# A fourth chunk's transposition leaves TensorE, a weight factor moves to ScalarE, and the written-out order is searched again

## The chip, the cores and the metric

The kernel runs on one core of a Trainium2 chip. The core has five engines with a queue of instructions each: TensorE (PE: matrix products; PEld in the profile is its loading of the stationary operand), VectorE (DVE), ScalarE (ACT), GpSimd (POOL) and SyncE (SP), which here issues all DMA transfers. Each works off its own queue in order, and waits where its data or its buffer come from another engine. The metric is the device time of one execution in microseconds. Most executions of a kernel agree within 0.3%.

## What is computed

The reference chains a gated linear attention and a two-layer block, all in 32 bits, with batch 4, 8 heads, 768 tokens, 48 values per head (384 in all) and 1536 hidden values:

```python
for t in range(S):                                   # 768 tokens, per batch and head
    state = alpha[:, :, t, :, None] * state + k[:, :, t] (outer) v[:, :, t]
    y[:, :, t] = q[:, :, t] @ state
x = y.transpose(0, 2, 1, 3).reshape(B, S, H * D)     # (4, 768, 384)
mu, var = mean and variance of x over its 384 values
xn = (x - mu) / np.sqrt(var + 1e-06) * g_ln
out = x + np.maximum(xn @ w_ch1, 0.0) @ w_ch2        # w_ch1 384x1536, w_ch2 1536x384
```

`w_ch1` and `w_ch2` arrive as 64-bit floats, all else as 32-bit floats.

## The kernel before, in words

**Chunks.** The 768 tokens are cut into six chunks of 128 (`c` = 0 to 5); with four batches (`b`) there are 24 blocks. `attention(c, b)` does one: logarithm of alpha, running sums as a product with a triangle (`lps`), exponentials, scaling of k and q on VectorE (`qk`), their transposition to `kT` and `qT`, scores (`aps`), masking into `at`, update of the state (`sums`, `mid`, `st`), and the output `yps`, which ScalarE copies to `x`. Then `x` is normalized to `xn` on ScalarE (on VectorE in chunk 0) without the factor g, and `xn` is transposed into `xT_of[c]`, the operand of the first layer.

**Two ways to transpose.** With `c < BY_DMA` (2) for q and k, and `c < X_BY_DMA` (4) for x, TensorE transposes: for x three 128x128 products with the unit matrix into a PSUM tile `xps` (line 530), which VectorE (chunk 0) or ScalarE (others) copies to `xT` (line 532). In later chunks VectorE transposes blocks of 32x32 in place (`xr`, line 536), four DMAs write the blocks to a DRAM tile `xd` in transposed places (line 540), and one DMA reads it back into `xT` (line 543).

**Weights.** Each weight matrix comes in six pieces of 768 values per partition (`pieces`: six of w1, then six of w2; turns `A` to `L`). `take_weights(i)` loads a piece as 64-bit words into one of three staging buffers `ws`, and `round_weights(i)` makes 32-bit floats of it. VectorE takes the fraction out (lines 219 and 221) and the exponent bits (line 223), ScalarE shifts and clamps the exponent (line 227), VectorE joins sign and exponent to a power of two (line 229), and then multiplies fraction and power. For w1 that last step also multiplies g, one value per row of w1; a row block has its own column of `g_part`, so there are three instructions of 256 columns (line 233). For w2 it is one instruction of 768 columns (line 236).

**The layers.** Chunk 0 is done plainly (`hidden`, line 567, and `project`, line 579). Chunks 1 to 5 use schemes of sums and fewer products. First layer: sums of blocks of w1 (`combine_first`) and of xT (`combine_x`, line 834), 15 products instead of 18 (`hidden_product`, line 857), then additions of the products into `hT` on VectorE and GpSimd, and the maximum with zero on ScalarE (line 907). Second layer: sums of blocks of w2 (`combine_weights`) and hT (`combine_hidden`, line 670), 20 products instead of 24 (`product`, line 683), additions into `ob` on VectorE (lines 693 and 696) and GpSimd (line 699), and the output DMA (`send`, line 558).

**The order.** Nothing is scheduled by a compiler. Every part is a Python generator, called a turn; each `yield` ends a step. `ORDER` is a string, and each of its letters runs the next step of one turn: `a` to `x` are the 24 attention blocks, `A` to `L` the weight pieces, `Y` `Z` `P` `Q` chunk 0's layers, `S` and `W` the sums of weights, `X` and `N` those of x and hidden values, `1` and `2` the two halves of the first layer's products, `R` and `U` the maxima, `M` the second layer, `O` the reloading of x. So the string fixes the order of the instructions on each engine, and of the DMAs in SyncE's queue; the waits between engines follow from the data.

```python
    with tc.manual_schedule():
        for turn in ORDER:
            next(turns[turn], None)
```

Of the kernel before, what the change touches and what calls it, by code (L numbers as in the profile page):

```python
# [11 lines left out]
FP32 = mybir.dt.float32  # L12
# [4 lines left out]
AOP = mybir.AluOpType  # L17
# [1 line left out]
EPS = 1e-6  # L19
STAGED = 3  # L20
BY_DMA = 2
X_BY_DMA = 4
SPLIT = 4
AHEAD = 2
G = 32
# [5 lines left out]


ORDER = (
    "bacabcadaacbcaadbcadabcababbebaccbadbaaBbccaedcbceAeeaaacbfecfBcdafddeaedbdeafae"
    "bcdccbfgadhAdcgCcdbebeebfhggdfgbfffbCdcgfgecdfchgdfhgabcddchdhAiiegjhacehedhhjfg"
    "biAdfidAeBhBijffYYiCjZZYYifZYlZCgjYDlYYjjZZYBZYgDieEgDgDjZZekEhZYGZgZigZGeeYgYgg"
    "fZYEhfGfkChihiYFYijfgEhgkhFZYhgYfghijgkFeZZlGZShfZYHlhHfYFYZeZHelYiZgllPmZkJIgJk"
    "PeiYjJIflHeSZIQgkIlYSjiPkffennSQlOKjLSnSjmSQhKnSjLnKPkiljnhSQnLkkjkWknkShOmPhkhl"
    "kOOhWlmmphmQmkmXjWQnXjlSQjPmkilXSXkP2OXWjXQjkjW2iXoSWX2oWX22Pi2mnol1j1mom2omSpoo"
    "l1XSpk2oW2m112p1m2pm11m1W211pp12O122r22jnn21lpnmnjSml1riOn2l12Rl111kqS1m21W1Rkp2"  # L40
    "o21mUXpq1mU2rUrnmj1rl2Rno2oomqonrormpokO1rNM2Mipin1op1ionoqUM2qp2W12RkMmNqiMoRtk"
    "UrpkqNM1NoMliMlNUMMNMNMKNqMlNorMWrnmtltNRMsqppMWNMriMMMpNlsqqqnoqttNttMtMsXMMssM"
    "sMNMNMX1oXXppMvstM2MXMMNMsppXoMXoqMsMMXM1nqqv11Xq1trMq2tqX21rn12v1r2ur2r222rvsqs"
    "svsu1rs1nuvvt2s11ss11p22rtsvosn2uropuXru222221uts212stnU1211u1121222Op1Rp2tRU21R"
    "Us1pXqU11x2tO2MM1vwMUM12xuRvu1vurNNNNwtOuuMwRxvNtxRNutwwMM2MOwNXwMNuXMMtNM1rMMMw"
    "qtXMMMxNUNxtMMsNMMMxXxMtXtrMMqMNrMXNvutMMwNuMMMNMMMxMLMOM11vvuq2X2O2wMus1wX11222"
    "2r2Xt1222w22utsqxvw2x2ww1vx21sX12121xwvq2O2x2w111u1uvU121w12s1wuRvx12U11J1q21R1U"
    "OvRxU121wMMu2xxsRNMw2NNMRM1MUNN2MMuUMqXN1MrNNRMNvMXNXMMMM2MMMxNM1uNXMMNMNMOXMXMv"
    "MMXOMMMXxNxwxMMvNMMMMMXMx21w1x222212v12w222x122w2212X11UX2212121121121wx111MU11X"
    "2RR2v1211212211R1URU211XOUM2XNRX1MX1RM2MXN2MXNXNMXXMXMMMN111U1MN1M1122MNM1MM2MM1"  # L50
    "11NNN121O11NM1MM21N1112N1122M1MMM12MM12N222M22M2RM1M2N22MM2MU1ON2M22M2UURR22RNNM"
    "MNM1MMOMRMNMUUM2ONMNNNMO2MMMUMNMMMMMRMMNNMMMNMNMMNMMMMMMMMNMNMMMMMMM"
)


# [1 line left out]
def kernel(  # L57
# [36 lines left out]
    nc = tc.nc  # L94
# [9 lines left out]
    NJ = DF // P  # L104
# [81 lines left out]
    g_part, zero_col = small[:, NF + 2:2 * NF + 2], small[:, 2 * NF + 2:]  # L186
# [22 lines left out]
    def round_weights(i):  # L209

        dst, _ = pieces[i]
        ws = staged.pop(i)
        words = ws.bitcast(INT32).rearrange("p a (c t) -> p a c t", t=2)
        lo, hi = words[:, :, :, 0], words[:, :, :, 1]
        ts, stt = nc.vector.tensor_scalar, nc.vector.scalar_tensor_tensor
        ts(out=dst.bitcast(INT32), in0=hi, scalar1=0x000FFFFF, scalar2=0x00100000,
           op0=AOP.bitwise_and, op1=AOP.bitwise_or)  # L220
        stt(out=dst, in0=lo.bitcast(UINT32), scalar=2.0 ** -32, in1=dst.bitcast(INT32),  # L221
            op0=AOP.mult, op1=AOP.add)
        ts(out=lo, in0=hi, scalar1=0x7FF00000, scalar2=None, op0=AOP.bitwise_and)
        yield
        if i == 0:
            nc.scalar.mul(g_part, g_col, 2.0 ** -20)
        nc.scalar.activation(out=lo, in_=lo, func=AFT.Relu, scale=8.0, bias=least)
        yield
        stt(out=hi, in0=hi, scalar=-(1 << 31), in1=lo, op0=AOP.bitwise_and,
            op1=AOP.bitwise_or)  # L230
        if i < NJ // 2:
            for f in range(NF):
                stt(out=dst[:, f], in0=dst[:, f], scalar=g_part[:, f:f + 1],
                    in1=hi[:, f].bitcast(FP32), op0=AOP.mult, op1=AOP.mult)
        else:
            stt(out=dst, in0=dst, scalar=2.0 ** -20, in1=hi.bitcast(FP32),  # L236
                op0=AOP.mult, op1=AOP.mult)

    def take_weights(i):
        if i < STAGED:  # L240
            load_weights(i)
            yield
        if pieces[i][1].dtype != FP32:
            yield from round_weights(i)
        yield
        load_weights(i + STAGED)
        yield
# [50 lines left out]
    def attention(c, b):  # L298
# [226 lines left out]
        if c not in xT_of:  # L525
            xT_of[c] = work.tile([P, NF, B, P], FP32, name="xT", tag="xT")
        if c < X_BY_DMA:
            xps = ps.tile([P, NF, P], FP32, name="xps", tag="bank", bufs=6)
# [440 lines left out]
```

## Time and profile before

| | |
|---|---|
| median of 3 runs | 420.69 us (420.14 to 421.5) |
| the profiled execution | 420.64 us |
| its span, first to last instruction | 418.9 us |
| busy TensorE / VectorE / ScalarE / GpSimd | 409.0 / 351.4 / 178.0 / 153.2 us |
| granted TensorE clock | 1.00 |
| moved by DMA | 59.52 MB, 133741 packets |

Busy times are unions of the instructions' intervals. Matrix products are pipelined: the duration of one (381 ns for 128x256) is longer than the distance to the next in a stream, so a busy TensorE need not be one at its peak. A 32-bit product appears as two records in the profile, a transposition as one. An engine that is idle away from the path that ends last costs nothing.

### The profile page before, as it was taken

How to read it: one execution, taken by the hardware profiler on the slowest of the kernel's cores; microseconds unless marked ns; L12 is line 12 of the kernel's file. 1: busy time of each engine (PE TensorE's matmuls, PEld its weight loads, DVE VectorE, ACT ScalarE, POOL GpSimd, SP SyncE). 2: the span in 40 equal slices, each digit the busy share in tenths (PEclk: the TensorE clock that was granted, in tenths of full speed). 3: DMA queues.
4: the chain of work that ended last, by engine and by line, in shares of the span. 5: the costliest groups of instructions: out<-in, count | busy, mean ns of one | idle time of the engine just before them, and what ended most of it. 6: DMA issues, size and time to landing. Idle time of an engine off the chain costs nothing.

```text
span 418.9 us, 11553 instructions
## 1 busy us (share of the span) xinstructions
PE 409.0 (98%) x4608; PEld 360.9 (86%) x4608; DVE 351.4 (84%) x713; ACT 178.0 (42%) x440; POOL 153.2 (37%) x169
## 2 busy tenths in 40 slices
PE   6998999999999999999999999999999999999996
PEld 4787888766678889998889999889998899999996
DVE  3999999999999989996888996688876767977873
ACT  5498456724243496414546612364313242014110
POOL 3011000003203990043395033493152940499123
PEclk9999999999999999999999999999999999999999
DMA  7998889987778778587784546433035200001201
GB/s 247 325 297 246 206 201 293 287 194 181 145 221 176 200 167 185 128 195 178 146 215 70 130 105 166 88 95 77 0 114 104 67 1 2 0 20 38 94 20 56
DMA packets 133741, 59.52 MB, mean 142 GB/s; under 512 B 90764, under 2 KB 129804, under 8 KB 133688
## 3 DMA queue, kind: packets, MB, share of 16 engines
q1 hardware_dynamic: 133688, 58.79, 55.1%
q8 instruction: 36, 0.59, 0.6%
q14 instruction: 17, 0.14, 0.1%
HBM read 42.17 MB, written 16.61 MB: 140 GB/s over the span
## 4 chain that ended last, share of the span: by engine, by line
PE 89%; DVE 4%; ACT 2%; DMA 2%; issue 1%; SPq 1%; POOL 0%; POOLq 0%; DVEq 0%
PE hps L857 31%; PE ops L683 30%; PE ops L579 8%; PE hps L567 8%; PE aps L405 3%; PE yps L463 3%; PE yps L467 2%; PE sums L432 2%; DMA rq<-in_q_dram 2%; PE xps L530 1%; PE tps L355 1%; PE aps L397 1%; PE lps L407 1%; SPq L132 1%; DVE w L221 0%
## 5 line engine op out<-in xcount | busy, mean ns | idle before, releaser
L699 POOL TENSOR_TENSOR ob<-ob,u 128x192 f32<-128x192 f32 x40 | 26.3, 668 | 64.5 <-DVE ob L696 48.3
L857 PE MATMUL hps<-sum,w 128*128 128x256 f32 x192 | 46.3, 381 | 0.0
L907 ACT ACTIVATE hT<-hT 128x512 f32<-128x512 f32 x48 | 28.8, 624 | 34.9 <-POOL hT L879 18.5
L447 POOL TENSOR_TENSOR mid<-mid,gate 112x192 f32<-112x192 f32 x20 | 11.4, 568 | 80.0 <-DVE mid L445 33.3
L683 PE MATMUL ops<-w,hT 128*128 128x192 f32 x224 | 40.5, 327 | 0.0
L857 PEld LDWEIGHTS hps<-sum,w 128*128 128x128 f32 x192 | 36.1, 190 | 5.0
L683 PEld LDWEIGHTS ops<-w,hT 128*128 128x128 f32 x224 | 37.1, 190 | 0.7 <-issue 0.2
L857 PE MATMUL hps<-xT,w 128*128 128x256 f32 x136 | 34.0, 380 | 0.0
L579 PE MATMUL ops<-w,hT 128*128 128x384 f32 x96 | 33.0, 491 | 0.0
L567 PE MATMUL hps<-xT,w 128*128 128x256 f32 x144 | 32.5, 382 | 0.0
L567 PEld LDWEIGHTS hps<-xT,w 128*128 128x128 f32 x144 | 27.0, 190 | 4.2
L683 PE MATMUL ops<-ws,sum 128*128 128x192 f32 x160 | 28.7, 327 | 0.0
L857 PEld LDWEIGHTS hps<-xT,w 128*128 128x128 f32 x136 | 25.5, 190 | 3.1
L683 PEld LDWEIGHTS ops<-ws,sum 128*128 128x128 f32 x160 | 26.5, 190 | 0.3
L579 PEld LDWEIGHTS ops<-w,hT 128*128 128x128 f32 x96 | 17.6, 190 | 10.7 <-DVE w L236 0.3
L693 DVE TENSOR_TENSOR ob<-ops,ob 128x192 f32<-128x192 f32 x50 | 17.3, 353 | 10.6 <-PE ops L683 6.5
L447 POOL TENSOR_TENSOR st<-st,gate 112x192 f32<-112x192 f32 x16 | 11.7, 729 | 37.3 <-DVE st L445 25.9
L683 PE MATMUL ops<-ws,hT 128*128 128x192 f32 x128 | 23.6, 328 | 0.0
L463 PEld LDWEIGHTS yps<-st,qT 48*64 48x64 f32 x320 | 19.9, 134 | 4.0 <-issue 2.0
L467 PE MATMUL yps<-vx,at 64*64 64x48 f32 x320 | 22.7, 219 | 0.0
L463 PE MATMUL yps<-st,qT 48*64 48x48 f32 x320 | 22.0, 220 | 0.6 <-ACT x L493 0.6
L405 PEld LDWEIGHTS aps<-qT,kT 48*64 48x64 f32 x576 | 19.0, 134 | 4.1 <-issue 0.8
(255 smaller groups left out, 1134.2 us busy)
## 6 DMA issues: line engine op xcount, KB each, us to landing
ws<-in_moe_w_ch_dram SPq DMA_DIRECT2D x12, 768.0 KB, 5.9
td<-tr SPq DMA_DIRECT2D x64, 96.0 KB, 3.1
vn<-in_v_dram SPq DMA_DIRECT2D x12, 384.0 KB, 4.3
kept<-x SPq DMA_DIRECT2D x20, 192.0 KB, 3.0
ob<-kept SPq DMA_DIRECT2D x20, 192.0 KB, 3.1
out_dram<-ob SPq DMA_DIRECT2D x19, 192.0 KB, 1.9
ra<-in_alpha_dram SPq DMA_DIRECT2D x16, 192.0 KB, 2.6
kT<-td SPq DMA_DIRECT2D x32, 96.0 KB, 4.2
```

The costliest lines, as they stand in the source:

```text
L405: nc.tensor.matmul(to, kT[rs, p, s], qT[rs, p, s], start=True, stop=True)
L432: nc.tensor.matmul(up[h, p], qk_of(c, b)[ts, 1, p, i, :h.stop - h.start], vn[ts, i, p], start=True, stop=True)
L447: nc.gpsimd.tensor_mul(new, new, by)
L463: nc.tensor.matmul(yps[i][halves[s], i, p], qT[rs, p, s], (now, mid)[s][rs, p], start=True, stop=r != i)
L467: nc.tensor.matmul(yps[r][halves[s], i, p], at[halves[r], p, s], by, start=r != i, stop=True)
L567: nc.tensor.matmul(hps, w1[:, j // 2, f, j % 2 * P:][:, :P], xT_of[0][:, f, bs], start=(f == 0), stop=(f == NF - 1))
L579: nc.tensor.matmul(ops_of[b], hT_of[c][:, j, b], w2[:, j], start=(j == 0), stop=(j == NJ - 1))
L683: nc.tensor.matmul(acc, lhs[:, j], rhs[:, j], start=(j == 0), stop=(j == NT - 1))
L693: nc.vector.tensor_add(x, acc, x)
L699: getattr(nc.gpsimd, f"tensor_{op}")(x, x, y)
L857: nc.tensor.matmul(acc[:, i], w, b, start=True, stop=True)
L907: nc.scalar.activation(out=x, in_=x, func=AFT.Relu)
```

## The change

Three things are changed. x of chunk 3 is no longer transposed by TensorE, but in the second way, as chunks 4 and 5 were. In `round_weights` for the pieces of w1, ScalarE multiplies g into the power of two (three instructions of 256 columns), and VectorE then multiplies fraction and power in one instruction of 768 columns, as for w2; two more steps (`yield`) stand around ScalarE's part. And `ORDER` is a new string, different from its fourth letter on, one line longer, so that lines of the changed kernel below it have numbers higher by one.

```diff
-X_BY_DMA = 4
+X_BY_DMA = 3
...
 ORDER = (
-    "bacabcadaacbcaadbcadabcababbebaccbadbaaBbccaedcbceAeeaaacbfecfBcdafddeaedbdeafae"
-    "bcdccbfgadhAdcgCcdbebeebfhggdfgbfffbCdcgfgecdfchgdfhgabcddchdhAiiegjhacehedhhjfg"
...
-    "MNM1MMOMRMNMUUM2ONMNNNMO2MMMUMNMMMMMRMMNNMMMNMNMMNMMMMMMMMNMNMMMMMMM"
+    "bacOabbccbaadbbacacacbacbdaacbabdadcbadacadbfacafdbdedabcfecdafCcafcBbebdcgaddab"
+    "hcbcdeffebbcebCcfeeBdeaecadhdbffcgdefagdghibcddAefbghhedgegeggchghhadAeggjhhgdci"
...
+    "U2MM2M221M2RU2RM2RMM2NNMNUMOM2NUM1MMM1MRNMMNMNNUNOMMMNMNMMMNMMNMMMNMMMMMMMMNMNMM"
+    "MMMM"
 )
...
         if i < NJ // 2:
+            yield
             for f in range(NF):
-                stt(out=dst[:, f], in0=dst[:, f], scalar=g_part[:, f:f + 1],
-                    in1=hi[:, f].bitcast(FP32), op0=AOP.mult, op1=AOP.mult)
-        else:
-            stt(out=dst, in0=dst, scalar=2.0 ** -20, in1=hi.bitcast(FP32),
-                op0=AOP.mult, op1=AOP.mult)
+                nc.scalar.mul(hi[:, f].bitcast(FP32), hi[:, f].bitcast(FP32), g_part[:, f:f + 1])
+            yield
+        stt(out=dst, in0=dst, scalar=1.0 if i < NJ // 2 else 2.0 ** -20, in1=hi.bitcast(FP32),
+            op0=AOP.mult, op1=AOP.mult)
```

More of the change, by code (lines that the diff above doesn't have):

```diff
@@ L33 @@
 ORDER = (
-    "bacabcadaacbcaadbcadabcababbebaccbadbaaBbccaedcbceAeeaaacbfecfBcdafddeaedbdeafae"
-    "bcdccbfgadhAdcgCcdbebeebfhggdfgbfffbCdcgfgecdfchgdfhgabcddchdhAiiegjhacehedhhjfg"
[L36 to L51, printed above, removed]
@@ L52 @@
-    "MNM1MMOMRMNMUUM2ONMNNNMO2MMMUMNMMMMMRMMNNMMMNMNMMNMMMMMMMMNMNMMMMMMM"
+    "bacOabbccbaadbbacacacbacbdaacbabdadcbadacadbfacafdbdedabcfecdafCcafcBbebdcgaddab"
+    "hcbcdeffebbcebCcfeeBdeaecadhdbffcgdefagdghibcddAefbghhedgegeggchghhadAeggjhhgdci"
+    "AihAAeBcAeCejBfffeYfiOZBiYiZkBAYeCZjZfYZYBiCYDZZCEDlDZDYYYEjlfjZDghjZfiEZYZggDeY"
+    "jZefEigYChkZYjeGYgEfYZGhFeieGgEhZfFkYFiFhgZZHOYhZHZFYhfgkiYYZgjGFkYfSgHfjhigYlSf"
+    "hSJklHZhYlIlllIfkZiZIKfjmiQJIKJgniSePYgeQPPkLlggnPjSLkjlKLjnhSlhnnPkjmSjOnnWjiSk"
@@ new lines @@
+    "kSWnlkmQkPhkpkQliWmhmhimSmQSlmhnPhWQmXkoXWjoijlSk2XWQiP1XjXkkXlXjQ22nWj2XSWm1noX"
+    "pmimlSookjlmooo2lSpi112pXp2221mn2kk1m1m1Oi2i11m22kS12ppp22oSm11jj1121q12122X2mnj"
+    "21ijmW1m12iRn12Ur2rO1lnpoO1m2mokOlRUnlpLU2orpm2rrRmrrnq21oooq1UrnWpo2oM1MpoUlmq1"
+    "RnpRMpqlWq1sMoNMqNMslMNN1otRrnMqMNpMMnlqWlUpMMNoNrrptMMonnntNMNWkmMMMpNNqkNqqqtt"
+    "tMsttNsMMMNsMqsMNNotqMproXMMsMsMOMMXMMpMoXnMvXXsMMqX2XM1vt1qr2OrqMX1X21qu122rp1t"
+    "11o211rq12u22vrrv1rsvssr2s2vss22sos2t2vt2usu2p2pUXtv1p12u2q11Unu1sOtR122uX11O1p1"
@@ new lines @@
+    "22Uw1u1w11s1RRt2211x12v2qMMNMoRNUMM22uNMRUNNRMpxMMNuvMuuwsrvtNwMMMwNMMNwxpMutnMm"
+    "UNNuwwsMsutMqxxtXxNNMnxMrswMMMxMMNMrMMMMNvqMMMNtMXX1sMMXXXwvvMOxM1v2X2X1w2t22X12"
+    "1212r121qwM1222wxuuqwxrw2t2r22u1x2rOX1Uxwv12v2v1O12xqUv111x1t1swu11RX12t221R112U"
+    "1ROtR2vxu22sU12MM1xsRwU1NMNxrMNN2MMMN1MNNRMMNv2NMqNutwuMMxMuMtMMMxMUNXMMwxNXMMxw"
+    "MM1xMMN2NXMxMXMvXXvxNMwXvMMNMMXMMXMM1xw1221w2221v122121O2X21222wu111v21w2uU222M2"
+    "2U1211X1111O11122RRUX1211u222O1112RM1UMXXX2NMXMXNO2MXUMRNRMM1XNXN21M21M12MM21NXR"
@@ L53 @@
+    "112M2N1UM1NMMNM1MN211M1J11N1M2M11211MMM1N1OX2MMNRKMM111112R2NM22NMNMM22O2M2M22MU"
+    "U2MM2M221M2RU2RM2RMM2NNMNUMOM2NUM1MMM1MRNMMNMNNUNOMMMNMNMMMNMMNMMMNMMMMMMMMNMNMM"
+    "MMMM"
 )
```

## The prediction

> **What bounds the kernel now.** I read the page first: totals, then the forty slices.
>
> ```profile
> PE 409.0 (98%) x4608; PEld 360.9 (86%) x4608; DVE 351.4 (84%) x713; ACT 178.0 (42%) x440; POOL 153.2 (37%) x169
> ...
> PE   6998999999999999999999999999999999999996
> ...
> DVE  3999999999999989996888996688876767977873
> ```
>
> TensorE (PE) is busy nearly throughout. VectorE (DVE) is just as full from slice 2 to slice 14, and looser afterwards. So there are two stages: up to some 150 us both engines can set the pace, later TensorE alone. Next I read busy times per ten microseconds (columns: stretch, its length, then busy us of PE, PEld, DVE, ACT, POOL with counts).
>
> ```profile
> 20.00:30.00 10.00, 9.85 (x222) 8.66 (x222) 9.86 (x18) 8.87 (x27) 1.35 (x2) 1.00 1.06 295
> 30.00:40.00 10.00, 8.13 (x197) 6.87 (x189) 9.90 (x23) 9.12 (x25) 1.74 (x3) 1.00 0.96 275
> 50.00:60.00 10.00, 10.00 (x158) 8.43 (x158) 9.83 (x18) 5.53 (x10) 1.02 (x2) 1.00 0.85 177
> 110.00:120.00 10.00, 9.38 (x212) 6.70 (x212) 10.00 (x23) 1.79 (x5) 0.83 (x1) 1.00 0.79 195
> 310.00:320.00 10.00, 10.00 (x54) 9.22 (x53) 4.93 (x11) 3.52 (x7) 3.06 (x5) 1.00 0.53 118
> ```
>
> In 30 to 40 and again in 110 to 120 TensorE falls short while VectorE stands at 9.9 and 10.0: there TensorE waits for VectorE. The granted clock is 1.00. Last, the groups that the change touches, and four steps of the chain of work that ended last.
>
> ```profile
> L530 PE MATMUL xps<-consts,xn 128*128 128x128 f32 x48 | 7.8, 278 | 1.6 <-DVE xn L519 1.6
> ...
> L532 ACT COPY xT<-xps 128x384 f32<-128x384 f32 x12 | 5.5, 472 | 6.8 <-PE xps L530 6.8
> ...
> L536 DVE STREAM_TRANSPOSE xr<-xn 128x384 f32<-128x384 f32 x8 | 4.5, 568 | 0.0
> ...
> L233 DVE SCALAR_TENSOR_TENSOR w<-w,small,ws 128x256 f32<-128x256 f32 x18 | 7.7, 482 | 0.2
> ...
> L236 DVE SCALAR_TENSOR_TENSOR w<-w,ws 128x768 f32<-128x768 f32 x6 | 5.9, 990 | 0.2
> ...
> L570 ACT ACTIVATE hT<-hps 128x256 f32<-128x256 f32 x24 | 8.8, 380 | 11.1 <-PE hps L567 11.1
> ...
> L523 ACT ACTIVATE xn<-x,few 128x384 f32<-128x384 f32 x20 | 14.2, 709 | 0.7
> ```
>
> ```profile
> 159.79 0.33 PE xps L530 x3
> ...
> 115.08 0.50 ACT x L493
> ...
> 415.38 0.56 POOL ob L699
> 415.96 0.36 DVE ob L693
> ```
>
> Three transposes of x take TensorE 0.33 us in its stream (the 278 ns of one are mostly pipeline). At 115 us TensorE waits on an activation that itself came late. The run ends with a GpSimd addition that releases the last VectorE addition.
>
> **How I follow TensorE.** I add up the pitch of its instructions in their order: 432 ns for a product of line 857 or 567 (0.86 us for two in the chain), 325 at line 683, 645 at line 579, 109 for a transpose, small attention products by the length of their clusters. That gives 400.3 us of work; start minus work done is its lateness. It reads 4.6 us after the loads, 9.6 once the first weights are used (work 30 us), 10.05 at work 75, 12.1 at 115, 13.5 at 155, 15.5 at 265, and no more afterwards. I do the same for VectorE (lateness 8.7, 9.7, 10.8 and 14.2 at work 30, 75, 115 and 155) and call "lead" the VectorE work that must be done ahead of a TensorE instruction minus the TensorE work ahead of it. Lateness of VectorE plus lead is a floor under TensorE's. In the kernel before the highest lead is 0.6 us in the opening, 0.0 at work 50 to 80, and -1.1 to 0.0 from 100 to 150: VectorE is the floor all along.
>
> **The change, part by part.** (1) Chunk 3 loses four times three transposes: 12 x 109 ns = 1.3 us of TensorE work, on the path, so -1.3. Its four ScalarE copies go too (4 x 0.47 = 1.9 us), which is off the path.
>
> (2) Each of those four x gets one VectorE transposition (568 ns row; 2.2 us in all), four DMA writes and one read. They stand between TensorE work 143 and 234, where VectorE still shows gaps, so I cost them at nothing; uncovered they are 2.2 us. SyncE's queue gets 20 issues more. One takes 0.43 to 0.47 us in the lines 540 and 543; before, its densest stretch of 10 us of TensorE work holds 26 issues, after 23. From the end of normalization to the data in place it was 0.33 + 0.47 us; by the rows of chunks 4 and 5 it becomes 0.57 + 4 x 0.47 + 1.8 (landing of the write) + 0.43 + 2.7 (landing of the read) = 7.4 us. The new order pays for that by distance: the last read of chunk 3 is issued at work 233.8, the first product that needs VectorE's sums of it stands at 239.3. The way between is 0.43 + 2.7 + 2.8 us (VectorE's work from the first such sum to the last needed) = 5.9 against 5.5. But SyncE runs ahead: for chunk 4 before, it issued the corresponding read 2.7 us earlier than TensorE's lateness would put it. So about 2.2 us are to spare, and I cost it at nothing.
>
> [...]
>
> (3) Weights: per piece of w1, three VectorE products (7.7 / 18 = 0.43 us each) become one (5.9 / 6 = 0.98). 18 x 0.43 - 6 x 0.98 = 1.8 us less VectorE work, in its full stage. Against that ScalarE multiplies three times per piece between two VectorE steps, so VectorE hands over and waits. No row shows this form. Bounds for one product: 0.38 (line 570, the same width) and 0.71 (line 523, wider, with a scale per row); I take 0.43, nearer the equal width. A trip is then 3 x 0.43 + two handovers of some 0.06 = 1.4 us, at most 2.3. The new order puts other VectorE work into that gap: 0.74 us at the first piece, 1.19 at the second, 3.15, 0.93, 3.4 and 2.9 at the others. Uncovered: 0.7 + 0.2 + 0.5 = 1.4 us, bounds 0.8 and 4.1. Queued behind the waiting VectorE step are the next piece's rounding and the masks of the scores; TensorE's first hidden products wait for it.
>
> [...]
>
> (4) The order. In the opening the masks of line 411 take scores that stand 4.1 us deeper in TensorE's work than the masks stand in VectorE's; before it was 2.4. With TensorE 4.9 late there and some 0.2 us until a product is in, VectorE leaves the place 4.1 + 4.9 + 0.2 = 9.2 us late, against 8.6 at work 20 before: 0.6 more. With the trips VectorE is 2.0 us later after the opening. Its lead over TensorE is 0.5 at work 31, -0.2 at 75, -1.8 to -2.2 at 100 to 120, -3.6 at 130 to 160: in the second half of its full stage it is 1.5 to 2.6 us less in the way. Floor at 75: 9.7 + 2.0 - 0.2 = 11.5 (before 10.05). At 115: 10.8 + 2.0 - 1.8 = 11.0, at 155: 14.2 + 2.0 - 3.6 = 12.6, against 13.5 before. Net -0.9; bounds +1 (the relief meets another wait) and -2.5 (trips covered).
>
> (5) After 155 lateness rose 2.0 by short waits on ScalarE, DMA and GpSimd. The kind of work is the same, so zero, bounds +1 and -1. At the end the sums of the fourth last product stand 0.65 us further from the last one, which takes the GpSimd addition off the chain: -0.3, bounds -0.6 and 0.
>
> Sum: -1.3 - 0.9 - 0.3 = -2.5. The profiled execution took 420.64 us (span 418.9 and 1.7 around it), the median is 420.69, so no correction: **418.1**.
>
> **Rivals.** *Transposes alone:* VectorE's relief goes into another wait, and only (1) counts: 419.3. For it: 13.5 to 15.5 came from many small waits. Against: VectorE at 10.0 in 110 to 120.
>
> *ScalarE's trip decides:* products of 0.71 us, 4.1 us uncovered, VectorE 4.7 late; floor at 155 is 14.2 + 4.7 - 3.6 = 15.3, 1.8 above before; with -1.3 and -0.3 that is 420.8. For it: ScalarE at 9.12 in 30 to 40, where the first trips fall. Against: from 40 us on it is half idle.
>
> *x late, the slower case:* SyncE issues in order; a write of chunk 3 waits behind another engine, and chunk 3's first products stand. The queue's own waits show one such:
>
> ```profile
> SPq L540 <- DVE xr L536: 8.0, 2, 7.5
> ```
>
> A wait of 7.5 us on that path, less 2.2 to spare, costs 5.3: 420.64 - 2.5 + 5.3 = 423.4. It makes the kernel slower from a delay of 2.2 + 2.5 + 1.3 = 6.0 us. Against it: such waits before cost TensorE nothing.
>
> That the change does less than it says I exclude: in the order of its instructions it has 2348 matmuls for 2360, 677 VectorE instructions for 685, 426 on ScalarE for 412, 410 DMAs for 390, as counted above.
>
> **How the numbers follow.** A measurement of this kernel tells 0.3% (1.3 us) from no change: 419.4 to 421.9 is "the same". Forecast 0.54 (own range 415.7 to 419.9), transposes alone 0.15, ScalarE's trip 0.16, x late 0.15. Faster: 0.48 of the first, half of the second, 0.03 of the third, in all 0.59. Slower: x late and 0.02 of the trip, 0.17. Same: the rest, 0.24. The range reaches down to the sum of the good bounds (-1.3 - 2.5 - 0.6 - 1.0 = -5.4, 415.2) and up over the trip's case with 0.8 us of later waits: 415.2 to 421.6; most of x late stays outside.
>
> **What would show it.** Right: 36 transposes at the line of 530; TensorE 9.9 or more at 110 to 120; VectorE gaps of 0.5 to 1 us before the single weight product of the first two pieces, released by ScalarE; no wait of TensorE for x of chunk 3 near 245 us; lateness about 14.6 at the end. Wrong: products of 0.6 us or more on ScalarE; TensorE idle for over 2 us near 245 us; VectorE full up to 160 us and TensorE waiting with it.

## The result, and the profile after

The changed kernel takes 433.02 us (median of 5 runs, 431.84 to 433.66); the kernel before, run beside it, 420.72 (5 runs). The ratio is 1.0286, 95% interval 1.0259 to 1.0313: 12.3 us slower, where 2.5 us faster was predicted. The profiled execution took 433.02 us, span 431.3. In e6 and e12 below a single execution stood over 1.5% above the fastest of its kernel; their times and ratios leave it out, but the profile of e6 is of that execution.

The page of the changed kernel, totals and slices (the last row shown is the granted clock):

```profile
PE 413.5 (96%) x4596; PEld 363.7 (84%) x4596; DVE 356.8 (83%) x705; ACT 184.5 (43%) x454; POOL 154.4 (36%) x169
...
PE   7978899899989999999999999998999999999997
...
DVE  4777999999989899996999987696974798667983
...
PEclk9979999999999999999999999998999999999999
```

The instruction counts differ by the numbers predicted (12 fewer on TensorE, 8 fewer on VectorE, 14 more on ScalarE). What is new is in the slices: VectorE, full from the second slice on before, stands at 7 in slices 2 to 4, and the clock row has a 7 and an 8 where before the granted clock was 1.00. The busy times by stretch (stretch, length, then PE, PEld, DVE, ACT, POOL, clock, DMA share, GB/s) put numbers on it:

```profile
20.00:30.00 10.00, 7.08 (x135) 6.46 (x136) 6.00 (x11) 5.09 (x17) 0.95 (x1) 0.82 0.98 289
30.00:40.00 10.00, 8.21 (x162) 7.18 (x161) 7.59 (x16) 7.78 (x24) 1.29 (x1) 0.84 0.86 247
...
110.00:120.00 10.00, 10.00 (x125) 6.30 (x125) 8.94 (x17) 3.50 (x11) 2.32 (x3) 1.00 0.71 137
290.00:300.00 10.00, 7.99 (x57) 7.12 (x49) 6.88 (x17) 3.56 (x8) 5.82 (x5) 0.83 0.45 117
```

In 110 to 120 the relief that the prediction expected can be seen: TensorE 10.00, VectorE 8.94 (before 9.38 and 10.00), though this stretch of time now holds work that came some 9 us earlier before. But from 20 to 40 us VectorE is busy for 13.6 us instead of 19.8, and at 290 there is a second hole. Added up as in the prediction, TensorE is 17.2 us late after the opening (before 9.6), 22.8 at work 155 (13.5) and 28.9 at the end (15.3). About 7.6 us are lost in the opening (work 0 to 30), 1.7 more by work 155, 4.3 behind that; the 1.3 us of transposes come off.

What stands in the opening is in the chain of work that ended last (start, us, what):

```profile
20.04 7.25 DMA gate<-row
27.38 0.37 DVE st L442
...
28.68 2.74 PE tps L356 x12
31.42 1.90 PE yps L459 x32
```

A transfer of 2 KB is on the chain for 7.25 us. The gate of a block of chunk 0 is the last token's row of its running decay: that row of ScalarE's `eq` goes to DRAM as `row` and comes back as a column (`gate`), and VectorE's product `st` (line 442) needs it. SyncE's queue shows how it comes to that (start, us, issue; the first two lines are of the kernel before, the others of the changed kernel, where the third is from the chain).

```profile
7.53 1.43 SPq L334 DMA_DIRECT2D row<-eq  x2
12.80 0.37 SPq L423 DMA_DIRECT2D gate<-row  x1
...
9.84 0.43 DMA row<-eq
...
15.59 0.39 SPq L424 DMA_DIRECT2D gate<-row  x1
```

Before, the `row` of the first two blocks goes out at 7.53 and 8.72 us, ahead of the loads of chunk 1's first half (9.00 to 10.70 us, 1.2 MB), and the gates follow at 12.8, 14.7, 17.7 and 22.5 us; VectorE waits for none. In the new sequence these loads go out at 7.05 to 8.60 us, and the second `row` behind them at 9.84. The first gate waits for that row (the wait that ended last by the profile, 2.7 us) and issues only at 15.59, and SyncE, whose last issue ended at 12.84, holds everything behind it: the data engines run dry from 15 to 18 us (GB/s in slices of 1 us from 0 to 40),

```profile
GB/s 0 25 292 254 177 210 376 378 379 395 383 375 372 375 307 54 1 12 210 396 281 197 148 335 329 378 357 320 301 246 338 310 292 108 111 303 207 225 362 214
```

and then the other gates (18.3, 20.0, 21.7 us) mix with 1.2 MB of chunk 1's second half (16.1 to 17.8) and two loads of weights of 768 KB (18.8 and 20.5 us; before 13.9 and 15.1). VectorE's queue behind the waiting product holds masks, scaling and the weights' rounding; TensorE's sums of the next block wait for it (2.9 us in two pieces, the longer 2.0), because the blocks of chunk 0 use one PSUM tile for their sums, one after the other. From 26.4 to 33.3 us the granted clock is 0.50: the 12 transposes of q and k at 28.7 take 2.74 us, where 16 took 1.99 us in the kernel before:

```profile
10.36 1.99 PE tps L355 x16
```

At 293 us the waits of the stretch 290 to 298 show the second place:

```profile
ACT hT L908 <- POOL hT L896: 3.2, 2, 1.8
PEld hps L858 <- ACT x L482: 2.3, 1, 2.3
...
PE hps L858 <- ACT x L482: 2.0, 1, 2.0
```

TensorE waits for a PSUM tile that ScalarE has not yet copied to `x`; that copy stands in ScalarE's queue behind two ReLUs (line 908) that wait for GpSimd's additions.

### The profile page after: what moved, and what is told of

Its sections match the earlier page's. It is cut to its first block, busy times and chain, and to the rows that moved or that the text cites. A ratio compares the mean times of both kernels' runs of the same rounds, so it can differ in the third digit from the quotient of the medians.

```text
span 431.3 us, 11569 instructions
## 1 busy us (share of the span) xinstructions
PE 413.5 (96%) x4596; PEld 363.7 (84%) x4596; DVE 356.8 (83%) x705; ACT 184.5 (43%) x454; POOL 154.4 (36%) x169
## 4 chain that ended last, share of the span: by engine, by line
PE 87%; DMA 4%; DVE 4%; issue 1%; ACT 1%; SPq 1%; POOL 1%; DVEq 0%; ACTq 0%
PE ops L684 30%; PE hps L858 28%; PE hps L568 7%; PE ops L580 7%; PE aps L406 3%; PE sums L433 2%; PE yps L464 2%; PE yps L468 2%; DMA gate<-row 2%; PE tps L356 1%; DMA rk<-in_k_dram 1%; PE yps L459 1%; DMA xT<-xd 1%; PE xps L531 1%; SPq L133 1%
## 5 line engine op out<-in xcount | busy, mean ns | idle before, releaser
L700 POOL TENSOR_TENSOR ob<-ob,u 128x192 f32<-128x192 f32 x40 | 27.8, 706 | 60.7 <-DVE ob L697 47.9
L448 POOL TENSOR_TENSOR mid<-mid,gate 112x192 f32<-112x192 f32 x20 | 12.6, 628 | 91.4 <-DVE mid L446 69.9
L908 ACT ACTIVATE hT<-hT 128x512 f32<-128x512 f32 x48 | 28.5, 624 | 38.1 <-POOL hT L880 13.9
L580 PE MATMUL ops<-w,hT 128*128 128x384 f32 x96 | 32.6, 489 | 0.0
L580 PEld LDWEIGHTS ops<-w,hT 128*128 128x128 f32 x96 | 17.8, 190 | 10.9
L684 PEld LDWEIGHTS ops<-ws,sum 128*128 128x128 f32 x160 | 26.4, 190 | 0.3
L684 PE MATMUL ops<-ws,hT 128*128 128x192 f32 x128 | 24.8, 339 | 0.0
L684 PEld LDWEIGHTS ops<-ws,hT 128*128 128x128 f32 x128 | 22.5, 199 | 0.5
L468 PE MATMUL yps<-vn,at 64*64 64x48 f32 x320 | 22.4, 220 | 0.5 <-issue 0.5
L448 POOL TENSOR_TENSOR st<-st,gate 112x192 f32<-112x192 f32 x16 | 10.5, 658 | 33.5 <-DVE st L446 33.5
```

What stands on the lines that cost most here:

```text
L448: nc.gpsimd.tensor_mul(new, new, by)
L468: nc.tensor.matmul(yps[r][halves[s], i, p], at[halves[r], p, s], by, start=r != i, stop=True)
L580: nc.tensor.matmul(ops_of[b], hT_of[c][:, j, b], w2[:, j], start=(j == 0), stop=(j == NJ - 1))
L684: nc.tensor.matmul(acc, lhs[:, j], rhs[:, j], start=(j == 0), stop=(j == NT - 1))
L700: getattr(nc.gpsimd, f"tensor_{op}")(x, x, y)
L908: nc.scalar.activation(out=x, in_=x, func=AFT.Relu)
```

## Experiments

Two theories at the start. A: the sequence of turns loses the time, in the opening (A1: gates behind loads) and at 293 us (A5). B: one of the two code changes loses it. `OLD` and `NEW` are the two strings of turns; ratios are to the kernel before, run in the same rounds.

**e1 and e1b: x over DRAM alone, in the old sequence.**

```diff
-X_BY_DMA = 4
+X_BY_DMA = 3
 ORDER = OLD with one turn more for each of m, n, o, p; first X of chunk 3 later
```

> The kernel before with one part of the change: x of chunk 3 goes by VectorE and over DRAM; the old sequence of turns, with one turn more for each of chunk 3's four blocks and the first combination of chunk 3's x moved some 46 turns back, behind the later arrival. Theory A (the order of turns costs the 12 us, this part gains its 12 transposes): 420.7 - 1.3 = 419.4 us, between 418.4 and 420.6. Theory B (the transfer of x is what costs): 423 us or more, with TensorE waiting for products of chunk 3 near 225 us.

431.5 us, 1.0256 [1.0203, 1.0309]: a miss for theory A. In the waits from 205 to 255 us:

```profile
DVE xr L536 <- DMA xd<-xr: 6.2, 1, 6.2
...
PE hps L857 <- DVE qk L327: 4.3, 1, 4.3
```

The second block's transposition got the buffer of the first, whose four writes stood in SyncE's queue behind `vn` and `vx`. In e1b that is mended by hand:

> Again the kernel before with x of chunk 3 over DRAM, in the old sequence of turns, but the second and third block's transposes on VectorE 18 turns apart and each block's writes issued at once behind its transpose, the first combination of x 51 turns back. In the first placement VectorE's second transpose waited 6.24 us for the buffer that the writes of the first had not yet left, and TensorE 4.41 us behind it. Theory A (that wait was the placement's, the part itself gains its transposes): 418.5 to 421.5 us, and no VectorE wait for a write of x. Theory B (a transfer of x costs wherever it stands in the old order): 425 us or more.

431.5 us again, 1.0252 [1.0202, 1.0301]. That wait is gone and others have come: the largest, 4.2 us of TensorE, is for the reads of q and k of chunk 5:

```profile
PE aps L405 <- DMA qT<-td: 4.2, 1, 4.2
```

In SyncE's queue from 216.7 to 227.7 us stand eight writes and three reads of x of chunk 3 (the writes 2.0 to 2.1 us a set of four), and the reads of q and k issue only behind them. So in the old sequence, at two hand-made placements, the way over DRAM costs 10 to 11 us. The traces show SyncE's issue time and a buffer as the waits, not the transfer (a write of x lands in 1.8 us in e1). This is the rival "x late" in another place. It is not what the changed kernel suffers: there TensorE's longest wait between 225 and 255 us is 0.2 us (a weight load), and it is for issue.

**e2: g on ScalarE alone, in the old sequence.**

```diff
         if i < NJ // 2:
+            yield
             for f in range(NF):
-                stt(out=dst[:, f], in0=dst[:, f], scalar=g_part[:, f:f + 1], ...)
+                nc.scalar.mul(hi[:, f].bitcast(FP32), hi[:, f].bitcast(FP32), g_part[:, f:f + 1])
+            yield
 ORDER = OLD with two turns more for each of A to F
```

> The kernel before with the other part alone: ScalarE multiplies g into the exponent word, in the old sequence of turns with two turns more for each of the six pieces of w1 (word and multiplication put a few turns ahead of the last product; ScalarE's exponent step of the second piece put beside that of the first). Theory A (the order costs the 12 us): between 419.5 and 422, since VectorE has 1.8 us less to do and each product waits some tenths of a microsecond for ScalarE. Theory B (ScalarE's trip is what costs): 424 us or more, the opening later by 3 us or more.

422.78 us, 1.0039 [1.0015, 1.0062]: 1.6 us slower (0.6 to 2.6), a little above A's range and far from B's 424. B falls for this part.

**e3: the new sequence alone.**

```diff
-X_BY_DMA = 3
+X_BY_DMA = 4
 round_weights as before
 ORDER = NEW without the parts' own turns
```

> The new sequence of turns with neither part: the turns that belong to the parts alone are taken out, VectorE multiplies g as before, x of chunk 3 is transposed on TensorE. Theory A (the order costs): 433.0 + 1.3 = 434.3 us, between 432.5 and 436, with VectorE waiting for the gates of chunk 0 as in the changed kernel (3 us or more in the opening) and TensorE at half clock behind it. Theory B (the parts cost): 424 us or less.

434.91 us, 1.0318 [1.0274, 1.0363]. The sequence alone has the whole loss. With both code changes in it the ratio is 1.0286, so they may gain some 1.3 us together, but the two intervals overlap. Theory A holds, with fewer gate waits than expected (1.4 us).

**e4: the old opening, the rest new.**

```diff
-ORDER = NEW
+ORDER = OLD[:162] + NEW without the turns that OLD[:162] has used
```

> The changed kernel with both parts; the first 162 turns (to about 38 us) are those of the old sequence, the rest are those of the new one in their order. Theory A1 (7.6 us are lost in the opening, by the gates of chunk 0 queued behind the bulk loads, and carried to the end): 433.0 - 7.6 = 425.4 us, between 423.5 and 427.5, with no VectorE wait for a gate and no half clock before 40 us. Rival A2 (what the opening loses is met again by later waits, the loss lies elsewhere in the order): 431 us or more.

428.55 us, 1.0171 [1.0121, 1.0221]: between the two forecasts. The gates' waits are gone, but ScalarE's product of the first piece is now bare (VectorE waits 1.4 us for line 235, TensorE 1.3 for VectorE), and a half-clock window follows at 42.9 us.

**e5, e6, e7: gates on another queue; the copy before the ReLUs; both.**

```diff
-            nc.sync.dma_start(gate[:, :ne], ...)                            # e5, e7
+            (nc.gpsimd if whole else nc.sync).dma_start(gate[:, :ne], ...)
-    "1ROtR2vxu22sU12MM1xsRw...                                              # e6, e7
+    "1ROt2vxxRu22sU12MM1sRw...
```

> The changed kernel, but the four small gate transfers of chunk 0 are issued from GpSimd's queue instead of SyncE's. Theory A1 (the opening loses its time because these 2 KB transfers stand behind 0.4 to 1.2 MB loads in one queue): VectorE waits for gates under 0.5 us (3.3 us in the changed kernel), no TensorE stall of 2.1 us near 23 us, no half clock at 26 to 33 us, and 433.0 - 5 = 428 us, between 425 and 430. Rival A3 (the data engines are full, so another queue does not help): gates land as late, 432 us or more. Rival A4 (the opening is late by its order of work on VectorE and not by the gates): gates on time, but 431.5 us or more.

> The changed kernel, but near 290 us ScalarE copies x of a block of chunk 5 out of PSUM before two ReLUs that wait for GpSimd, instead of behind them (two turns move). Theory A5 (TensorE's stall of 2.16 us at 293.3 us comes from that order, and the half clock at 296.1 to 299.5 us from the stall): both gone, 433.0 - 2.2 - 1.7 = 429.1 us, between 428 and 431. Rival: TensorE is held there by something else next (VectorE's sums, the ReLUs themselves), and less than 1.5 us is gained: 431.5 us or more.

> Both edits together: gates of chunk 0 from GpSimd's queue, and the copy of x ahead of the two ReLUs near 290 us. If the two losses are separate, the gains add: 433.0 - 5 - 3.9 = 424.1 us, between 421 and 427. If later waits take the opening's gain back, 429 us or more.

e5: 436.55 us, 1.0344 [1.0285, 1.0404], worse. GpSimd is idle, yet its first gate issues at 16.0 us, and all four are slow:

```profile
POOL gate L424 <- DMA row<-eq: 11.9, 1, 11.9
```

```profile
gate<-row POOLq DMA_DIRECT2D x4, 2.0 KB, 5.8
```

The first view is GpSimd's waits, the second the DMA issues (size, median us to landing). GpSimd waits until 16.0 us for the second `row`, the other half of the way through DRAM, issued at 10.3 us behind the same 1.2 MB of loads; and then 2 KB take 5.8 us. So rival A3 fits: from GpSimd's queue, while the data engines still moved 160 to 406 GB/s, the four gates took 5.2 to 6.8 us to land, against 4.4 by the profile of the kernel before, and VectorE waited 5.3 us for one, where it waited 3.3 us for three in the changed kernel.

e6: 430.65 us, 1.0214 [1.016, 1.0268]; the forecast was 429.1, between 428 and 431. e7: 432.38, 1.027 [1.0221, 1.0319], far from its forecast of 424.1, with the loss of e5 in it. The hole at 293 us is gone; the clean pair for its price is e8 and e9 below.

**e8, e9: loads behind the gates, without and with the copy moved.**

```diff
-            load(c + 1, b // 2, "akq")
+            load(c + 1, b // 2, "a" if (c, b) == (0, 3) else "akq")   # k, q: new turn z
-    "badacadbfacafdbdedabcfecdafCcafcBbebdcgadd abhcbc...
+    "badacadbfacafdbdedabcfecdafCcafc bebdcgaddzBabhcb...
```

> The changed kernel, but in the opening the loads of k and q of chunk 1's second half and one load of weights (1.5 MB in all) are issued behind the last gate of chunk 0 instead of ahead of three of them; all gates stay on SyncE's queue. The run with the gates on GpSimd's queue showed 5.2 to 6.8 us from issue to landing, so another queue did not help while the loads filled the data engines. Theory A1b (2 KB transfers wait behind the bytes already asked for, whatever the queue): VectorE waits for gates under 0.8 us in the opening (3.3 us in the changed kernel), no TensorE stall over 1.2 us between 20 and 35 us, and 433.0 - 5 = 428 us, between 425 and 430.5. Rival A4 (the opening is late by its order of work on VectorE): gates on time, but 431.5 us or more.

> The same, and the copy of x of a block of chunk 5 ahead of the two ReLUs near 290 us, which alone took away the stall at 293 us and the half clock behind it. If the losses are separate, 428 - 3.9 = 424 us, between 421.5 and 427; if the opening is late by its order of work, 427.5 to 430 us.

e8: 433.09 us, 1.0277 [1.0247, 1.0306], no gain. e9: 430.6, 1.023 [1.0193, 1.0268]; both missed their forecasts. Moving the copy is worth 2.5 us by the two medians, not 3.9. The intervals of the two overlap, but the ratio falls in all three pairs that differ by this copy: by 0.0047 here, by 0.0072 from the changed kernel to e6, by 0.0074 from e5 to e7. And TensorE is full there:

```profile
290.00:300.00 10.00, 10.00 (x113) 9.15 (x112) 8.23 (x18) 3.89 (x8) 7.44 (x6) 1.00 0.40 100
```

In e9 VectorE waits 0.2 us for gates instead of 3.3. Yet the first product of the hidden layer (line 568) starts at 47.6 us, after 48.3 in the changed kernel and 39.7 before. The gate's wait was removed and the time was not: VectorE now waits 4.0 us for weights (line 220), one load of which I had put behind the gates. The chain of e9:

```profile
19.69 4.42 DMA gate<-row
...
26.37 6.71 DMA rq<-in_q_dram
```

My first theory, that the gates are the cause, falls in that form: they were the wait that ended last, and others stood right behind.

**e10: everything removed that I could name.**

```diff
-ORDER = NEW
+ORDER = OLD[:162] + NEW without the turns used, copy before the ReLUs (e6); g on VectorE
```

> The first 162 turns of the old sequence, then the new one; g is multiplied by VectorE as before (the wait for ScalarE's product cost TensorE 1.42 us and a half-clock window at 41 to 46 us in the run with the old opening), x of chunk 3 goes over DRAM, and the copy near 290 us stands ahead of the two ReLUs. If the opening (7.6 us) and the place near 293 us (3.9 us) are all that the new sequence loses, 433.0 - 7.6 - 3.9 = 421.5 us, between 420 and 423.5; if the rest of the new sequence loses too, 425 us or more.

422.91 us, 1.0049 [1.0029, 1.007], inside the forecast (a second run, e10b below, came out higher). First hidden product at 40.8 us, granted clock 1.00, and no transfer among the long pieces of its chain up to 48 us.

**e11: products that fill the waits.**

```diff
+        if whole and b >= 2:
+            for _ in range(10 if b == 2 else 6):
+                nc.tensor.matmul(sums[1]...[:, :P], zero[:, :R], zero, start=True, stop=True)
...
+        if (c, r, n) == (3, 0, 12):          # ten more, the same
```

> The changed kernel with matrix multiplications that nobody reads: 10 and 6 ahead of the two products of the opening that wait for VectorE behind a gate, and 10 ahead of the product that waits at 293 us, each 128 x 112 by 128 x 128, into a bank that is free there. They fill waits and take none away. Theory C (waits of some 2 us inside one 3.41 us window halve the granted clock for the next window): no half clock at 26 to 33 us nor at 296 to 299.5 us, and 433.0 - 1.7 - 2 = 429.3 us, between 427.5 and 431. Rival (the clock is not what costs; TensorE waits as long for others): 432 us or more.

431.61 us, 1.0249 [1.0223, 1.0275]. The clock is 1.00 in both places, and one half-clock window (46.0 us) is left:

```profile
PEclk9999899999999999999999999999999999999999
```

The gain is 1.4 us where 3.7 were expected, and the interval overlaps with the changed kernel's (1.0259 to 1.0313). Over all executions, by their mean clocks, the changed kernel has 2.8 half-clock windows of 3.41 us in an execution (one lowers the mean clock by 0.004), e11 has 1.2 and the kernel before 0.3. Among executions of one kernel, each window more goes with 1.1 us more (0.8 to 1.3, from 156 executions of all kernels here). By that estimate the half clock goes with some 2.7 of the 12.3 us. It is an upper estimate, since the waits that come ahead of a half clock cost time themselves.

**e12: the bytes in another order.**

```diff
-    "badaca dbfacafdbdedabcfecdafCcafcBbebdcgadd  abhc...   (A1 some 45 turns later)
+    "badacCadbfacafdbdedabcfecdaf cafcBbebdcgaddzAabhc...   (and e6, and load as in e8)
```

> The changed kernel with the copy near 290 us ahead of the two ReLUs, and in the opening the order of the transfers changed: one load of weights goes out ahead of the first gate, into the gap of 15 to 18 us in which the data engines stood idle; k and q of chunk 1's second half and the load of the weights needed first go out right behind the last gate. VectorE's instructions keep their order. Theory B1 (the order of the bytes makes VectorE idle): waits of VectorE for gates and weights under 1 us together in the opening (3.3 us in the changed kernel, 4.0 in the run with loads behind the gates), first hidden product at 43 to 45 us instead of 48.3, and 430.6 - 4 = 426.6 us, between 424.5 and 428.5. Rival B2 (VectorE's order of work): no wait for gates or weights, but others in their place; first hidden product past 46 us and 429.5 us or more.

428.93 us, 1.02 [1.0155, 1.0244], past the upper end of B1's forecast (428.5) and under B2's 429.5; first hidden product at 45.5, between the two. No wait for weights, 1.9 us for one gate. So this run decides for neither. Its chain has again two late transfers of little data and a load:

```profile
9.93 6.11 DMA row<-eq
16.10 3.56 DMA gate<-row
...
25.89 8.81 DMA ra<-in_alpha_dram
```

**e13 and e10b: x of chunk 3 on TensorE again, beside its partner.**

```diff
-X_BY_DMA = 3
+X_BY_DMA = 4
 ORDER = e10's, m to p with two turns (transposes, copy) in place of three
```

> The variant with the old opening, g on VectorE and the copy ahead of the ReLUs, but x of chunk 3 transposed by TensorE and copied by ScalarE as before (12 transposes more). If the way over DRAM gains its transposes and costs nothing in the new sequence: 1.3 us more than the partner, so 424.2 us if that is 422.9, between 423.4 and 425. If the way over DRAM costs TensorE something there: less than 0.5 us more than the partner, or faster.

> The variant with the old opening, g on VectorE, x of chunk 3 over DRAM and the copy ahead of the ReLUs, run once more as the partner on the same chip: 422.9 us, between 422.2 and 423.7.

426.15 against 424.36 us on one chip (1.013 [1.0094, 1.0165] and 1.0085 [1.0053, 1.0117]): the way over DRAM gains 1.8 us in the new sequence behind the old opening; 1.3 were predicted. The single executions of the two spread over 2 us each, so the gain is uncertain by some 1.5 us to each side. Both times lie above their forecasts: e10b is 4.05 us over the kernel before, its twin e10 was 1.5.

**e14, e15, e16: where in the opening.**

```diff
+ORDER = OLD[:80] + ...      # e14, else as e10
+ORDER = OLD[:120] + ...     # e15
+ORDER = NEW up to the first Y + OLD's rest, neither code part   # e16
```

> The quiet variant (old opening, g on VectorE, copy ahead of the ReLUs; 422.9 and 424.4 us in two runs), but only the first 80 turns (to about 24 us) are the old ones. If the loss lies in the first 24 us (gates and order of loads): 423 to 425 us, first hidden product by 41.5 us. If it lies in VectorE's order of work behind that: 427 to 430 us, first hidden product past 44 us.

> The same with the first 120 turns (to about 31 us) of the old sequence. If the loss lies in the first 24 us, as the run with 80 turns; if it lies evenly over VectorE's order of work between 24 and 48 us, between the two, some 425 to 427 us.

> The kernel before (neither part), but up to the first hidden product its turns are those of the new sequence, the rest the old ones. If the opening's loss is the sequence's own and stays to the end: 421 + 5 to 7 = 426 to 428 us. If later work of the old sequence takes it back: 423 us or less.

e14: 426.29 us, 1.0127 [1.0099, 1.0156]; e15: 424.49, 1.0079 [1.0049, 1.011], as e10b within its interval; e16: 426.94, 1.0146 [1.0109, 1.0183], 5.3 us over the kernel before, as forecast. e14 lies between its two forecasts. With 120 turns of the old sequence the opening's loss is gone, so it is made in the first 31 us, and e16 shows that the old rest does not take it back. In e14 one load of weights came late; its issue stands at 20.45 us, as one does in the changed kernel (20.47):

```profile
20.45 9.15 DMA ws<-in_moe_w_ch_dram
```

Put together, one profiled execution each (VectorE's busy and idle time are those up to the first hidden product, from VectorE's first instruction at 0.9 us on; "on the chain" are transfers of over 3 us that land between 10 us and that product):

| kernel | first hidden product, us | VectorE busy / idle, us | transfers on the chain |
|---|---|---|---|
| before | 39.7 | 31.9 / 6.9 | none |
| e13 | 40.4 | 32.6 / 6.9 | gate 4.68 |
| e10 | 40.8 | 32.4 / 7.5 | none |
| e15 | 40.9 | 33.0 / 7.0 | none |
| e10b | 41.7 | 33.1 / 7.6 | none |
| e4 | 42.6 | 32.4 / 9.3 | v 6.64 |
| e14 | 43.4 | 32.0 / 10.5 | weights 9.15 |
| e16 | 45.4 | 33.1 / 11.5 | gate 7.21, weights 6.69 |
| e12 | 45.5 | 33.1 / 11.5 | row 6.11, gate 3.56, alpha 8.81 |
| e3 | 45.6 | 32.7 / 11.9 | v 7.49, weights 8.15 |
| e11 | 46.9 | 34.2 / 11.8 | weights 7.04, q 5.91 |
| e8 | 47.3 | 33.1 / 13.3 | v 9.09, weights 7.67 |
| e9 | 47.6 | 33.2 / 13.5 | gate 4.42, q 6.71 |
| changed | 48.3 | 33.2 / 14.1 | gate 7.25 |

Kernels with the same opening show how far one execution can be trusted: e10, e10b and e13 differ by 1.3 us, the changed kernel and e11 (the same but for the filling products) by 1.4, and not the same transfers stand on their chains. So differences of that size between rows mean nothing.

What the runs show: the opening of the new sequence makes the loss (e10 and e15 without it, e16 with it alone), and VectorE idles more there, while its work ahead of the product grows by 0.1 to 1.3 us (2.3 in e11). What is read from the traces: where the product is late, large or small transfers stand on the chain, different ones from kernel to kernel. Their lengths do not rank the kernels (e12 has the longest), and one stands on e13's chain without harm. That the transfers are the cause, and not the new order of VectorE's and ScalarE's work in the same stretch, fits the traces but was not separated: e12, the run meant for it, came out between its two theories. That the root is the second `row` at 9.84 us and the three dry microseconds behind it is read from the traces too (e12 has it: the row of 9.93 us in its chain, 16.10 its first gate); a run with that row alone moved ahead was not made.

## Why the prediction was wrong

**Step (4), the order, failed.** "0.6 more" for the opening measured 7.6. The floor under TensorE was built from VectorE's work and its lead over TensorE; no transfer was in it, and neither was a wait of VectorE. In the changed kernel VectorE idles for 7.2 us more ahead of the first hidden product, 3.3 of it directly for gates. I had compared SyncE's queue near chunk 3 and by the count of issues in its densest stretch, and not transfer by transfer in the opening, where only the string moved it. The two sequences could have been compared there without a run: in the new one the second row stands behind 1.2 MB of loads that it preceded before, and the first weights behind 1.2 MB that they preceded. Net -0.9 at work 155 was forecast with a floor of 12.6; it measured 22.8, 9.3 more than before. The half clock, which the profile of before never showed, added to it: some 2.7 us at most by the estimate at e11, and 1.4 us measured there, not clear of noise. What remains open is how much of the 7.6 is due to late transfers and how much to the new order of the engines' work around them.

**Step (5), "zero, bounds +1 and -1", failed too.** Lateness grew by 4.3 us more than before behind work 155. Moving one ScalarE copy ahead of two ReLUs gave about 2.5 us back (e8 to e9). I had called the kind of work the same; the order in ScalarE's queue was not, and I had not looked for the instruction that a late ReLU holds up. The gain of 0.3 at the end cannot be told apart here. The sum's end, 418.1, rests on these two steps; its lateness of 14.6 at the end measured 28.9.

**Steps (1) and (2) held.** 36 transposes are left; no wait for x of chunk 3; 1.8 us gained in the new sequence (e13 to e10b, uncertain by 1.5) for 1.3 predicted. "I cost it at nothing" is right only in a sequence that leaves SyncE the room: in the old one, placed by hand, it cost 10 to 11 us in e1 and e1b.

**Step (3) held in size.** The groups of the changed kernel (count, busy us, mean ns, idle before):

```profile
L237 DVE SCALAR_TENSOR_TENSOR w<-w,ws 128x768 f32<-128x768 f32 x12 | 11.7, 975 | 1.8 <-ACT ws L235 1.5
...
L235 ACT ACTIVATE ws<-ws,small 128x256 f32<-128x256 f32 x18 | 8.3, 542 | 2.2 <-DVE ws L230 2.2
```

VectorE's uncovered wait is 1.5 us in three pieces (0.70, 0.35, 0.50), 1.4 predicted (0.7, 0.2, 0.5). One product lasts 542 ns and three in a row 1.37 us on the chain, 0.46 each, for the 0.43 taken; the two handovers of the first trip took some 0.03 us each, for the 0.06 taken. On VectorE's own count the part should have gained 0.4 us (1.8 less 1.4); in the old sequence it cost 1.6 us (e2), and in that profile TensorE ran one window from 35.7 us at half clock. So the size was right, and its worth on the path of the old sequence was not.

**The rivals.** The slower rival named SyncE's order as the mechanism and put it at chunk 3. The kind fits the traces, the place and size do not: 5.3 us were priced there, and the loss sat in the opening, where VectorE's next products wait for 2 KB.

**What stays open.** The separate prices are 5.3 us for the opening (e16), 1.6 for g (e2), 2.5 for the copy (e8, e9), less 1.8 for x, in all 7.6. e10, which has the first three removed and the gain of x kept, is still 1.5 us over the kernel before in one run and 4.05 in the other (e10b), so the rest of the new sequence costs about 3.3 to 5.9. That makes 10.9 to 13.5, beside 12.3 measured. The prices come from different sequences and each is uncertain by 1 us or more, so the sum shows that no large piece is missing, and no more. Where the rest's 3.3 to 5.9 us sit was not tried; the trace of e10 puts most of them between 60 and 155 us of TensorE's work, in short waits on ScalarE. None of the variants is faster than the kernel before.

## What to carry to other kernels

When a written-out order changes, compare every queue at every stage, the DMA queue first: follow each small transfer that a product waits for (here a row that becomes a column by way of DRAM), and count the bytes asked for ahead of it. Taking away the wait that ended last shows its price only if nothing stands right behind it; here other transfers did, and only putting the whole opening back (e10, e15) or moving it alone (e16) gave the price. Repeat the variant whose place in the argument is largest: e10 and its twin differ by 2.5 us against the kernel before. A step that is free in one sequence cost 10 us in another here, so a part and the order made for it are judged together.

## What the runs showed of the hardware

In e5 the four gates of 2 KB took 5.8 us in the median to land, issued from GpSimd's queue while the data engines moved 160 to 406 GB/s (slices of 0.5 us from 16 to 24 us). Issued from SyncE's queue they took 4.4 us by the profile of the kernel before; single ones on the chain lasted 3.56 (e12), 4.42 (e9), 7.21 (e16) and 7.25 us (the changed kernel).

The granted clock fell to one half for whole windows of 3.41 us: in the changed kernel for two (6.83 us) from 26.4 us on and for one from 296.1. In the window ahead of each, TensorE was busy for only 1.43 and 1.40 us and idle for 58 and 59%, nearly all of it in one wait of 2.0 us. Cut into steps of 3.413 us along the recorded changes of the clock, the traces of the two kernels have 239 windows at full clock: the two with 58 and 59% idle were followed by half clock, the 237 others, with 53% at most, were not. That is no rule for other kernels, and the sum of idle time alone does not decide: from 20 to 40 us TensorE is idle for 2.01 us in e2, 2.00 in e10 and 3.59 in e3, and of these only e2 shows half clock there (mean 0.91, the others 1.00). With waits filled by products that nobody reads (e11) the clock was 1.00 in both places, and its executions have 1.2 half-clock windows on average instead of 2.8.
